# Image shift's product with the value weight: formed on VectorE and summed by a short strip, instead of a full strip on TensorE

## The chip, the cores and the metric

One core of a Trainium2 chip runs the whole kernel. The metric is device microseconds of one execution; the median of three runs of the kernel before is 116.47 us (116.44 to 116.78).

## The reference

One attention block of a diffusion transformer with two streams, image (2 x 256 tokens) and text (2 x 32 tokens), both of width D = 1152, all in bfloat16. `c` has one row for each of the two images of the batch (called image 0 and image 1 below).

```python
mod_i = (silu(c) @ wmod_img).reshape(B, 6, 1, D)      # mod_t likewise from wmod_txt
shi, sci, gai = mod_i[:, 0], mod_i[:, 1], mod_i[:, 2]  # shift, scale, gate
hi = layernorm(x_img) * (1 + sci) + shi               # ht likewise
qkvi = hi @ wqkv_img                                   # qkvt likewise
q, k, v = concat(text, image) of the three thirds
p = softmax(q @ k^T * D ** -0.5)
a = p @ v
out_i = x_img + gai * (a_img @ wo_img)                 # out_t likewise
```

What the change touches is a rearrangement of the value path. The kernel multiplies the value weight `w_v_i` with the normalized and scaled image tokens before the shift is added. The missing part of v is the same for all tokens of one image: the row `shi @ w_v_i`. Since each row of p sums to one, that row may be added once behind the attention (`sv`, added to `aT`), if the text's v has it subtracted (`v_t` and `svn`). So the kernel needs `shi @ w_v_i`: two rows of 1152 numbers, each a sum over 1152 products.

## The kernel before

Weights are 1152 x 1152 blocks, loaded as `[128, 9, 1152]` (a partition holds nine rows, indexed `kt`; 2.65 MB each). There are fourteen of them. They come in by DMAs that the SP queue issues in one fixed order, into six buffers of the pool `w` that are used in turn: a load waits on SP until the block that had its buffer is no longer read, and everything behind it on SP waits too. `w_sc_i` and `w_v_i` have two of the six buffers first.

The order of work is written out by hand, and each engine works through its own list:

- Start: layer norm of the image tokens, scale columns, and v without its shift (L244, L395, L344), until about 31.7 us. The image's shift is formed as a *strip* (below), read back as columns into `mod_i`, and added to `hT_i` (L223, L226, L230); the last evacuation of v on VectorE (L153) ends at 33.7 us.
- Query stage, `qk_img(w_q_i, 0)`: nine output blocks `j` of 128 columns, each nine matmuls of 512 tokens (L445). The first three blocks run together, the others one by one. `qk_evac` moves each block from PSUM to `qkT`, alternating between VectorE (L429) and ScalarE (L431).
- Three strips, L452 to L454: `tsh` (text shift, called the shift strip), `tsc` (text scale, the scale strip) and `svr` (the image shift's product with `w_v_i`, the third strip). A strip (`strip_rows`) multiplies two rows with a whole weight block. It uses only 32 of TensorE's columns at a time, so that four column groups take four pieces of the output side by side: 9 x 4 matmuls of 256 columns (L368) and 9 of 128 (L372), then one evacuation to SBUF by `evac`, which alternates between VectorE (L153) and ScalarE (L155). `svr` uses `shT32`, a copy of the shift columns that GpSimd makes. Behind it GpSimd negates a part (`svn`, L456) and issues six DMAs that spread the rows through DRAM (`ssc`) to the text partitions (`v_t`, L459 and L463).
- Key stage, `qk_img(w_k_i, 1, hooks)`: as the query stage. The hooks put other work ahead of a block: `txt_norm` ahead of block 0 (layer norm of the text `x_t` into `xn_t`, L162 to L174, then a table load for the exponential on ScalarE, L474), `all_cols` ahead of block 3 (the *selection*: six small matmuls, L384 and L386, turn the strips `tsh` and `tsc` into columns, and VectorE writes them to `mod_t`, L389 and L391), `txt_transposes` ahead of block 6 (nine small matmuls, L489, transpose the text; VectorE multiplies and adds into `hT_t`, L490 and L492).
- Text projections of query and key (L503), scores and softmax (L529, L516, L521), text scores and gate (L542), text value (L604), transposes of p, attention output (L673; `sv` is added in L686 and L688), output projection (L765), text output (L783), stores.

PSUM tiles of the tag `mm` take seven banks in turn: in the key stage a new block or strip can start only when the tile seven before it has been evacuated.

## Time and profile before

| | |
|---|---|
| runs, median of three | 116.47 us (116.44 to 116.78) |
| span of the profiled execution | 114.4 us |
| TensorE busy | 109.5 us, 96% of the span |
| VectorE, ScalarE, GpSimd busy | 53.3, 34.3, 27.9 us |
| DMA | 40.89 MB, 357 GB/s over the span, 396 to 416 GB/s from 20 to 94 us |
| TensorE clock granted | 1.00 throughout |

The profiled execution has no time of its own besides its span, from the first to the last instruction of the program; the runs' times lie 2.1 us above it (116.47 less 114.4). Times in the views are microseconds from the start of the span; mean durations of one instruction are nanoseconds. PE is TensorE's matmuls, PEld its weight loads, DVE VectorE, ACT ScalarE, POOL GpSimd, SP the queue that issues the loads. A line such as L445 is a line of the kernel file.

### The profile page before, as it was taken

To read this page: it belongs to the slowest core of one execution; us is meant where nothing else is said; L and a number is where in the kernel's file an instruction comes from. 1 tells how busy PE (TensorE), PEld (TensorE's weight loads), DVE (VectorE), ACT (ScalarE), POOL (GpSimd) and SP (SyncE) were. 2 spreads that over 40 slices of the span, in tenths; PEclk is the share of its full clock that TensorE was granted. 3 is DMA by queue.
4 is the path that set the end of the run, shared out by engine and by line. 5 is a ranking of instruction groups with operands and counts; after the bars stand their busy time and mean duration, and the time that the engine had idled before them with its cause. 6 is when DMAs were issued, how large, how long until landed. Compare 5 with 4: busy or idle time off the path is not lost.

```text
span 114.4 us, 2934 instructions
## 1 busy us (share of the span) xinstructions
PE 109.5 (96%) x1248; PEld 65.7 (57%) x1255; DVE 53.3 (47%) x137; ACT 34.3 (30%) x84; POOL 27.9 (24%) x59
## 2 busy tenths in 40 slices
PE   5998999999999999999999999999999999999990
PEld 1364564544944444486444546987687565667670
DVE  1699820452470402211832342136665803998571
ACT  2829660342370321021360122116555700001000
POOL 7000102540140000002224000001450560999100
PEclk9999999999999999999999999999999999999999
DMA  3999999999999999999999999999999999962142
GB/s 72 347 389 323 366 380 401 413 412 413 413 405 404 412 413 405 409 412 410 405 408 413 396 411 413 404 416 399 412 407 406 407 413 397 389 241 103 39 156 69
DMA packets 22744, 40.89 MB, mean 357 GB/s; under 512 B 1279, under 2 KB 6539, under 8 KB 22731
## 3 DMA queue, kind: packets, MB, share of 16 engines
q1 hardware_dynamic: 21648, 39.64, 90.8%
q0 software_dynamic: 608, 0.88, 2.1%
q10 hardware_dynamic: 475, 0.18, 0.7%
q8 instruction: 10, 0.16, 0.5%
q14 instruction: 3, 0.02, 0.1%
HBM read 39.36 MB, written 1.34 MB: 356 GB/s over the span
## 4 chain that ended last, share of the span: by engine, by line
PE 87%; DMA 7%; SPq 3%; issue 1%; DVE 0%
PE qkps L445 30%; PE ps L765 16%; PE va L244 10%; DMA w_sc_i<-in_wmod_img_dram 7%; PE aps L673 5%; PE ps L503 4%; PE sps L529 4%; PE gps L368 4%; PE ops L783 2%; PE ps L344 2%; SPq L93 2%; PE ps L395 2%; PE ps L604 2%; PE mps L204 1%; PE gps L738 1%; PE sps L542 1%
## 5 line engine op out<-in xcount | busy, mean ns | idle before, releaser
L445 PE MATMUL qkps<-hT_i,t 128*128 128x512 bf16 x158 | 35.4, 379 | 0.2
L445 PEld LDWEIGHTS <-t 128*128 128x128 bf16 x162 | 15.6, 98 | 18.3
L765 PE MATMUL ps<-t,aT 128*128 128x384 bf16 x99 | 16.4, 326 | 0.0
L765 PEld LDWEIGHTS <-aT 128*128 128x128 bf16 x117 | 11.0, 98 | 6.9 <-issue 0.5
L244 PE MATMUL va<-w_v_i,hT_i 128*128 128x512 bf16 x60 | 14.1, 378 | 0.2
L749 POOL TENSOR_TENSOR w_og<-t,gb 128x384 bf16<-128x384 bf16 x9 | 8.8, 1018 | 4.2 <-issue 4.2
L244 PEld LDWEIGHTS <-hT_i 128*128 128x128 bf16 x63 | 5.8, 97 | 6.5 <-POOL hT_i L228 0.5
L771 DVE TENSOR_TENSOR tmp<-ps,gb 128x384 bf16<-128x384 f32 x11 | 6.0, 549 | 6.1 <-DMA gb<-mod_scratch 4.4
L429 DVE TENSOR_SCALAR qkT<-qkps 128x512 bf16<-128x512 f32 x4 | 2.8, 692 | 11.6 <-PE qkps L445 11.6
L139 PE MATMUL wps<-wz 128*128 128x512 bf16 x16 | 6.3, 551 | 1.2 <-DVE wz L127 1.2
L162 DVE BATCH_NORM_STATS2 stats<-x_i 128x6 f32<-128x384 bf16 x12 | 5.9, 538 | 2.6 <-DMA x_i<-in_x_img_dram 2.6
L431 ACT ACTIVATE qkT<-qkps 128x512 bf16<-128x512 f32 x5 | 2.9, 596 | 13.5 <-PE qkps L445 13.5
L153 DVE CAST qkT<-qkps 128x512 bf16<-128x512 f32 x4 | 2.8, 692 | 7.7 <-PE qkps L445 7.7
L228 POOL TENSOR_SCALAR hT_i<-hT_i,mod_img 128x256 bf16<-128x256 bf16 x5 | 2.5, 514 | 15.6 <-DVE mod_img L213 12.3
L155 ACT CAST qkT<-qkps 128x512 bf16<-128x512 f32 x5 | 2.8, 587 | 10.6 <-PE qkps L445 10.6
L523 POOL COPY px<-pb 128x64 bf16<-128x64 bf16 x4 | 0.9, 238 | 19.8 <-DVE pb L521 19.8
L772 DVE TENSOR_TENSOR o<-tmp,x_i 128x384 bf16<-128x384 bf16 x11 | 5.4, 488 | 0.4
L456 POOL TENSOR_SCALAR svn<-svr 128x128 bf16<-128x128 bf16 x1 | 0.3, 300 | 20.6 <-DVE svr L153 20.6
L686 DVE TENSOR_SCALAR aT<-aps,sv 128x288 bf16<-128x288 f32 (+2 forms) x11 | 4.3, 456 | 2.0 <-PE aps L673 2.0
L503 PEld LDWEIGHTS <-t 128*128 128x128 bf16 x162 | 4.9, 98 | 0.2
L503 PE MATMUL ps<-hT_t,t 128*128 128x64 bf16 x162 | 4.9, 193 | 0.0
L673 PE MATMUL aps<-pT,v_i 128*128 128x288 bf16 (+2 forms) x44 | 4.8, 264 | 0.0
(159 smaller groups left out, 143.8 us busy)
## 6 DMA issues: line engine op xcount, KB each, us to landing
t<-in_wmod_txt_dram SPq DMA_DIRECT2D x3, 2592.0 KB, 21.5
t<-in_wmod_img_dram SPq DMA_DIRECT2D x2, 2592.0 KB, 22.3
t<-in_wqkv_img_dram SPq DMA_DIRECT2D x6, 864.0 KB, 13.6
t<-in_wqkv_txt_dram SPq DMA_DIRECT2D x2, 2592.0 KB, 17.2
t<-in_wqkv_txt_dram SPq DMA_DIRECT2D x3, 864.0 KB, 13.6
t<-in_wo_img_dram SPq DMA_DIRECT2D x1, 2592.0 KB
t<-in_wo_txt_dram SPq DMA_DIRECT2D x3, 864.0 KB, 15.5
w_v_i<-in_wqkv_img_dram SPq DMA_DIRECT2D x4, 576.0 KB, 8.2
```

The costliest lines, as they stand in the source:

```text
L139: nc.tensor.matmul(ps[:], lhsT=wz[:, 0:P], rhs=wz[:], start=True, stop=True)
L162: nc.vector.bn_stats(stats[0:np_, k, :], x_ap[:, k * CH:(k + 1) * CH])
L244: nc.tensor.matmul(ps[:], lhsT=hT_i[:, kt, i * P:(i + 1) * P], rhs=w_v_i[:, kt, half * VW:(half + 1) * VW], start=(kt == 0), stop=(kt == K ...
L368: nc.tensor.matmul(gps[32 * g:32 * g + 32, 0:RC], lhsT=lhs[:, kt, :], rhs=wt[:, kt, g * RC:(g + 1) * RC], start=(kt == 0), stop=(kt == KT ...
L445: nc.tensor.matmul(pss[j - j0][:], lhsT=wq[:, kt, j * P:(j + 1) * P], rhs=hT_i[:, kt, :], start=(kt == 0), stop=(kt == KT - 1))
L503: nc.tensor.matmul(ps[:, j - j0, :], lhsT=wq[:, kt, j * P:(j + 1) * P], rhs=hT_t[:, kt, :], start=(kt == 0), stop=(kt == KT - 1))
L529: nc.tensor.matmul(sps[:], lhsT=qkT[:, ft, b, q0:q0 + P], rhs=qkT[:, KT + ft, b, :], start=(ft == 0), stop=(ft == KT - 1))
L673: nc.tensor.matmul(bank[:, off:off + c1 - c0], lhsT=lhsT, rhs=rhs, start=(first[id(bank)] == n), stop=(final[id(bank)] == n))
L749: nc.gpsimd.tensor_mul(w_og[:, dt, 0:CH], w_o_i[:, dt, NG0:D], gb[:, B - 1, NG0:D])
L765: nc.tensor.matmul(ps[:, 0:cw], lhsT=aT[:, dt, t0:t0 + P], rhs=rhs, start=(dt == DTS[0]), stop=(dt == DTS[-1]))
L771: nc.vector.tensor_mul(tmp[:, 0:cw], ps[:, 0:cw], gb[:, b, cs])
L772: nc.vector.tensor_add(o[:, cs], tmp[:, 0:cw], x_i[:, i, cs])
```

## The change

The third strip is replaced. VectorE multiplies row block `kt` of `w_v_i` with the shift column of that block, one scalar per partition, and adds up over `kt` in float32: for each image nine instructions on `[128, 1152]`, the first a product alone (`tensor_scalar`), the other eight a product and a sum (`scalar_tensor_tensor`). What is left is a sum over the 128 partitions. The sum `sacc` is split into a bfloat16 high part (a copy on ScalarE) and a low part (the difference, on VectorE), and `shift_strip` adds up both parts of both images over the partitions with a stationary operand of ones: 16 matmuls of 256 columns and 4 of 128, instead of 36 and 9.

All products of image 0 and two of image 1 stand in VectorE's list ahead of the query stage's evacuations, which are all given to ScalarE; the low part of image 0 and the other seven products of image 1 stand between query and key stage. The high part of image 0 stands on ScalarE ahead of query block 5; that of image 1 ahead of the key evacuations.

The strips move from before the key stage to ahead of its block 6 (hook 6: `tsh`, `tsc`, short strip, then `svn` and the six DMAs). `txt_norm` moves from block 0 to block 3, and the low part of image 1 is formed inside it; the text is normalized in place. The selection moves from block 3 to block 7, and the text transposes from block 6 to block 8, the last.

`w_v_i`, which is now read until the products end, gets a home of its own ("V"), which `w_ga_i` takes over afterwards; the pool `w` has five buffers instead of six. `w_k_i` is loaded ahead of `w_sh_t` and `w_sc_t` instead of behind them. `qkT` becomes two tiles; the key's shares its place with `sacc` of image 0. Several small tiles share places, and paddings keep the large homes at multiples of 256 bytes.

```diff
-    wpool = ctx.enter_context(tc.tile_pool(name="w", bufs=6))
+    wpool = ctx.enter_context(tc.tile_pool(name="w", bufs=5))
...
-    w_v_i = wpool.tile([P, KT, D], bf, tag="w", name="w_v_i")
+    w_v_i = act.tile([P, KT, D], bf, tag="V", name="w_v_i")
...
-    nc.gpsimd.tensor_copy(shT32[:, :, 0:B], mod_i[:, 0:KT, :])
-
+    w_k_i = load_w(wqkv_img, D, K3)
     w_sh_t = load_w(wmod_txt, 0)
     w_sc_t = load_w(wmod_txt, D)
-    w_k_i = load_w(wqkv_img, D, K3)
...
-    w_ga_i = load_w(wmod_img, 2 * D)
+    w_ga_i = load_w(wmod_img, 2 * D, home="V")
...
-    qkT = act.tile([P, 2 * KT, B, NTOK], bf, tag="Q")
+    saccs = [act.tile([P, D], f32, tag=t, name="sacc") for t in ("K", "sacc")]
+    qkTs = [act.tile([P, KT, B, NTOK], bf, tag="Q", name="qT")]
     def qk_evac(out_ap, in_ap, blk):
         if blk == 0:
-            if evac_idx[0] % 2 == 0:
-                nc.vector.tensor_scalar_mul(out_ap, in_ap, SCALE)
-            else:
-                nc.scalar.mul(out_ap, in_ap, SCALE)
-            evac_idx[0] += 1
+            nc.scalar.mul(out_ap, in_ap, SCALE)
...
+    def shift_products(b, k0, k1):
+        for kt in range(k0, k1):
+            ap = mod_i[:, kt, b:b + 1]
+            if kt == 0:
+                nc.vector.tensor_scalar(saccs[b][:], w_v_i[:, kt, :], ap, None, op0=ALU.mult)
+            else:
+                nc.vector.scalar_tensor_tensor(saccs[b][:], w_v_i[:, kt, :], ap, saccs[b][:], op0=ALU.mult, op1=ALU.add)
+    def shift_high(b):
+        sparts[0, b] = work.tile([P, D], bf, tag="o", bufs=3, name="shi")
+        nc.scalar.copy(sparts[0, b][:], saccs[b][:])
+    def shift_low(b):
...
+        nc.vector.tensor_sub(lo[:, 0:D], saccs[b][:], sparts[0, b][:])
+    def shift_strip():
+        gps = ps_mm.tile([P, RC + P], f32, tag="mm")
+        terms = [(n, b) for b in range(B) for n in range(2)]
+        for m, (n, b) in enumerate(terms):
+            for g in range(NGG):
+                nc.tensor.matmul(gps[32 * g:32 * g + 32, 0:RC], lhsT=ones32[:, b, :], rhs=sparts[n, b][:, g * RC:(g + 1) * RC],
+                                 start=(m == 0), stop=(m == len(terms) - 1), tile_position=(0, 32 * g))
+        for g, (n, b) in enumerate(terms):
+            nc.tensor.matmul(gps[32 * g:32 * g + 32, RC:RC + P], lhsT=ones32[:, b, :], rhs=sparts[n, b][:, NGG * RC:D],
+                             start=True, stop=True, tile_position=(0, 32 * g))
+        g_sb = work.tile([P, RC + P], bf, tag="svr", bufs=1, name="svr")
+        evac(g_sb[:], gps[:])
+        return g_sb
...
-    qk_img(w_q_i, 0, hooks={})
-    tsh = rows_for_cols(w_sh_t, "tsh")
-    tsc = rows_for_cols(w_sc_t, "tsc")
-    svr = rows_for_cols(w_v_i, "svr", lhs=shT32)
+    shift_products(0, 0, KT)
+    shift_products(1, 0, 2)
+    qk_img(w_q_i, 0, hooks={5: lambda: shift_high(0)})
+    shift_low(0)
+    shift_products(1, 2, KT)
+    shift_high(1)
+    qkTs.append(act.tile([P, KT, B, NTOK], bf, tag="K", name="kT"))
...
+    def row_strips():
+        strips["tsh"] = rows_for_cols(w_sh_t, "tsh")
+        strips["tsc"] = rows_for_cols(w_sc_t, "tsc")
+        svr = strips["svr"] = shift_strip()
...
     def txt_norm():
-        ln_apply(x_t[:, :], P, xn_t[:, :], *ln_std(ln_stats(x_t[:, :], P), P))
+        lns = ln_std(ln_stats(x_t[:, :], P), P)
+        shift_low(1)
+        ln_apply(x_t[:, :], P, x_t[:, :], *lns)
...
-    qk_img(w_k_i, 1, hooks={0: txt_norm, 3: all_cols, 6: txt_transposes})
+    qk_img(w_k_i, 1, hooks={3: txt_norm, 6: row_strips, 7: all_cols, 8: txt_transposes})
```

More of the change, by code (lines that the diff above doesn't have):

```diff
@@ L71, in w_view, with load_w @@
         return src.rearrange("(kt p) n -> p kt n", p=P)
-    def load_w(src, c0, ksplits=((0, KT),)):
-        t = wpool.tile([P, KT, D], bf, tag="w")
+    def load_w(src, c0, ksplits=((0, KT),), home=None):
+        t = wpool.tile([P, KT, D], bf, tag="w", name="t") if home is None else act.tile([P, KT, D], bf, tag=home, name="w_home")
         for (k0, k1) in ksplits:
@@ L129 @@
     nc.gpsimd.memset(sT32[:], 0.0)
-    shT32 = const.tile([P, KT, 32], bf)
-    nc.gpsimd.memset(shT32[:], 0.0)
+    ones_full = const.tile([P, B * 32 + 96], bf)
+    ones32 = ones_full[:, 0:B * 32].rearrange("p (b c) -> p b c", b=B)
+    nc.gpsimd.memset(ones32, 0.0)
+    for b in range(B):
+        nc.gpsimd.memset(ones32[:, b, b:b + 1], 1.0)
     sTw_full = const.tile([P, KT * NT + 96], bf)
@@ L377, in rows_for_cols @@
         gps = strip_rows(wt, sT32 if lhs is None else lhs)
-        g_sb = work.tile([P, RC + P], bf, tag=nm, bufs=1, name=nm)
+        g_sb = work.tile([P, RC + P], bf, tag={"shr": "svr", "tsc": "garow2", "tsh": "of"}[nm], bufs=1, name=nm)
         evac(g_sb[:], gps[:])
@@ L422 @@
     gsc = tc.dram_tile([B, D], bf, name="mod_scratch")
-    qkT = act.tile([P, 2 * KT, B, NTOK], bf, tag="Q")
+    saccs = [act.tile([P, D], f32, tag=t, name="sacc") for t in ("K", "sacc")]
+    qkTs = [act.tile([P, KT, B, NTOK], bf, tag="Q", name="qT")]
     def qk_evac(out_ap, in_ap, blk):
         if blk == 0:
-            if evac_idx[0] % 2 == 0:
-                nc.vector.tensor_scalar_mul(out_ap, in_ap, SCALE)
-            else:
-                nc.scalar.mul(out_ap, in_ap, SCALE)
-            evac_idx[0] += 1
+            nc.scalar.mul(out_ap, in_ap, SCALE)
         else:
             evac(out_ap, in_ap)
+    sparts = {}
+    def shift_products(b, k0, k1):
[9 more added lines that the diff above has]
+    def shift_low(b):
+        if b == 0:
+            lo = work.tile([P, D], bf, tag="o", bufs=3, name="slo")
+        else:
+            lo_full = act.tile([P, D + 32], bf, name="slo_full")
+            lo = lo_full[:, 0:D]
+        sparts[1, b] = lo
+        nc.vector.tensor_sub(lo[:, 0:D], saccs[b][:], sparts[0, b][:])
[12 more added lines that the diff above has]
+        return g_sb
     def qk_img(wq, blk, hooks):
@@ L447, in qk_img @@
             for j in range(j0, j1):
-                qk_evac(qkT[:, blk * KT + j, :, 0:NI], pss[j - j0][:].rearrange("p (b n) -> p b n", b=B), blk)
-    qk_img(w_q_i, 0, hooks={})
-    tsh = rows_for_cols(w_sh_t, "tsh")
-    tsc = rows_for_cols(w_sc_t, "tsc")
-    svr = rows_for_cols(w_v_i, "svr", lhs=shT32)
+                qk_evac(qkTs[blk][:, j, :, 0:NI], pss[j - j0][:].rearrange("p (b n) -> p b n", b=B), blk)
+    shift_products(0, 0, KT)
[5 more added lines that the diff above has]
+    qkTs.append(act.tile([P, KT, B, NTOK], bf, tag="K", name="kT"))
     svn = const.tile([P, P], bf)
-    nc.gpsimd.tensor_scalar(svn[:], svr[:, RC:RC + P], -1.0, 0.0, op0=ALU.mult, op1=ALU.add)
     ssc = tc.dram_tile([B, NM], bf, name="shift_scratch")
-    for b in range(B):
-        nc.gpsimd.dma_start(ssc[b, :].rearrange("(q j) -> q j", q=NGG), svr[b:P:32, 0:RC])
-    for g in range(2):
-        for b in range(B):
-            r = 32 * (2 * g + b)
-            nc.gpsimd.dma_start(v_t[r:r + NT, :], ssc[b, g * VW:(g + 1) * VW].partition_broadcast(NT))
+    strips = {}
+    def row_strips():
+        strips["tsh"] = rows_for_cols(w_sh_t, "tsh")
+        strips["tsc"] = rows_for_cols(w_sc_t, "tsc")
+        svr = strips["svr"] = shift_strip()
+        nc.gpsimd.tensor_scalar(svn[:], svr[:, RC:RC + P], -1.0, 0.0, op0=ALU.mult, op1=ALU.add)
+        for b in range(B):
+            nc.gpsimd.dma_start(ssc[b, :].rearrange("(q j) -> q j", q=NGG), svr[b:P:32, 0:RC])
+        for g in range(2):
+            for b in range(B):
+                r = 32 * (2 * g + b)
+                nc.gpsimd.dma_start(v_t[r:r + NT, :], ssc[b, g * VW:(g + 1) * VW].partition_broadcast(NT))
     mod_t = const.tile([P, 2, KT, B], f32, name="mod_txt")
@@ L468 @@
     hT_t = act.tile([P, KT, NTT], bf)
-    xn_t = act.tile([P, D], bf)
     def txt_norm():
-        ln_apply(x_t[:, :], P, xn_t[:, :], *ln_std(ln_stats(x_t[:, :], P), P))
+        lns = ln_std(ln_stats(x_t[:, :], P), P)
+        shift_low(1)
+        ln_apply(x_t[:, :], P, x_t[:, :], *lns)
         junk = small.tile([P, 1], f32, bufs=1)
@@ L477, in all_cols @@
         ctp = ps_sm.tile([P, 2, NCOL + B], f32, tag="sm")
-        for k, rows in enumerate((tsh, tsc)):
+        for k, rows in enumerate((strips["tsh"], strips["tsc"])):
             select_cols(rows, ctp[:, k, :])
@@ L488, in txt_transposes @@
             for kt in range(k0, k1):
-                nc.tensor.matmul(tpt[:, kt - k0, :], lhsT=xn_t[:, kt * P:(kt + 1) * P], rhs=pick, start=True, stop=True)
+                nc.tensor.matmul(tpt[:, kt - k0, :], lhsT=x_t[:, kt * P:(kt + 1) * P], rhs=pick, start=True, stop=True)
             nc.vector.tensor_mul(hv[:, k0:k1], tpt[:, 0:k1 - k0, :].rearrange("p k (b t) -> p k b t", b=B),
@@ L504 @@
                                      start=(kt == 0), stop=(kt == KT - 1))
-            qk_evac(qkT[:, blk * KT + j0:blk * KT + j0 + jn, :, NI:NTOK],
+            qk_evac(qkTs[blk][:, j0:j0 + jn, :, NI:NTOK],
                     ps[:, 0:jn, :].rearrange("p j (b n) -> p j b n", b=B), blk)
@@ L528, in scores_img @@
         for ft in range(KT):
-            nc.tensor.matmul(sps[:], lhsT=qkT[:, ft, b, q0:q0 + P], rhs=qkT[:, KT + ft, b, :],
+            nc.tensor.matmul(sps[:], lhsT=qkTs[0][:, ft, b, q0:q0 + P], rhs=qkTs[1][:, ft, b, :],
                              start=(ft == 0), stop=(ft == KT - 1))
@@ L541, in scores_txt_and_gate @@
             for b in range(B):
-                nc.tensor.matmul(sps[NT * b:NT * (b + 1), :], lhsT=qkT[:, ft, b, NI:NTOK], rhs=qkT[:, KT + ft, b, :],
+                nc.tensor.matmul(sps[NT * b:NT * (b + 1), :], lhsT=qkTs[0][:, ft, b, NI:NTOK], rhs=qkTs[1][:, ft, b, :],
                                  start=(ft == 0), stop=(ft == KT - 1), tile_position=(0, NT * b))
@@ L582, in softmax_txt @@
         nc.vector.reduce_max(nmx[0:q, :], sps[0:q, :], axis=AX.X, negate=True)
-        e = work.tile([P, NTOK], f32, tag="e", bufs=1)
+        e = work.tile([P, NTOK], f32, tag="of", bufs=1, name="e")
         rs = small.tile([P, 1], f32, tag="rst", bufs=1)
@@ L629, in p_transposes @@
         svp = ps_sm.tile([P, NCOL + B], f32, tag="sm", name="svp")
-        select_cols(svr, svp)
+        select_cols(strips["svr"], svp)
         nc.vector.tensor_copy(pX[:], pX_ps[:, NT:NTOK + 2 * NT])
```

## The prediction

> **What bounds the kernel now.** I read the page's first part and the chain of waits by line, then the chain in order of time, then a table of stretches, then VectorE's groups by form and its timeline, and last the weight loads' issues.

> ```profile
> PE 109.5 (96%) x1248; PEld 65.7 (57%) x1255; DVE 53.3 (47%) x137; ACT 34.3 (30%) x84; POOL 27.9 (24%) x59
> ...
> PE 87%; DMA 7%; SPq 3%; issue 1%; DVE 0%
> ```

> TensorE is busy 96% of the span and is 87% of the chain that ended last; the DMA and SP shares (10%) lie before 12 us, where the first weights come in. What shortens the kernel is TensorE work taken away after that, as long as no new wait opens.

> The chain in order of time (start, length, what):

> ```profile
> 42.83 6.42 PE qkps L445 x29
> 49.25 1.10 PE gps L368 x36
> 50.35 0.16 PE gps L372 x9
> 50.51 0.98 PE gps L368 x36
> 51.49 0.11 PE gps L372 x8
> 51.60 0.98 PE gps L368 x30
> 52.59 0.22 PE gps L372 x8
> 52.80 0.76 PE qkps L445 x3
> ...
> 70.81 4.72 PE ps L503 x162
> ```

> The three strips fill 49.25 to 52.80 without a gap: 3.55 us, 1.18 each. In the table of stretches (us, then busy us of PE, PEld, DVE, ACT, POOL) TensorE is full before and behind them, while VectorE has room:

> ```profile
> 31.70:49.25 17.55, 17.44 (x85) 7.82 (x88) 4.76 (x13) 4.10 (x9) 1.15 (x3) 1.00 1.04 408
> ...
> 52.80:70.80 18.00, 17.89 (x101) 8.45 (x103) 7.56 (x18) 4.03 (x7) 3.63 (x7) 1.00 1.04 408
> ```

> The DMAs run at 408 GB/s all the while, so a load that starts late could become a second bound.

> **The strip.** Removed: the third strip, 36 matmuls of 256 columns and 9 of 128. Four column groups run side by side, so 36 are nine rounds: 0.98/9 to 1.10/9 = 0.11 to 0.12 us a round. Added: 16 matmuls of 256 columns (four rounds, 0.44 to 0.49) and 4 of 128 in one round (9 take 0.22 in three, so 0.07): about 0.53. TensorE saves 1.18 - 0.53 = **0.65 us**. The other two strips only move. Moving them puts three transitions elsewhere and adds none.

> **The products on VectorE.** 18 instructions of 1152 elements, and no row has one. The nearest, by form (operation, out<-in, count, busy us, mean ns of one):

> ```profile
> L162 DVE BATCH_NORM_STATS2 stats<-x_i 128x6 f32<-128x384 bf16 x12 | 5.9, 538 | 2.6 <-DMA x_i<-in_x_img_dram 2.6
> ...
> L686 DVE TENSOR_SCALAR aT<-aps,sv 128x288 bf16<-128x288 f32 x7 | 3.4, 511 | 2.0 <-PE aps L673 2.0
> ...
> L174 DVE TENSOR_SCALAR xn_i<-x_i,mv,rstd 128x1152 bf16<-128x1152 bf16 x4 | 2.3, 578 | 0.1
> ...
> L521 DVE TENSOR_SCALAR pb<-e,rs 128x288 bf16<-128x288 f32 x4 | 1.5, 370 | 0.1
> ...
> L573 DVE TENSOR_TENSOR v_t<-ps,v_t 128x512 bf16<-128x512 f32 x1 | 0.7, 692 | 0.2 <-PE ps L604 0.2
> ...
> L686 DVE TENSOR_SCALAR aT<-aps,sv 128x64 bf16<-128x64 f32 x2 | 0.6, 276 | 0.0
> ```

> L686 grows by (511-276)/224 = 1.05 ns an element and has 0.21 us fixed, with a scalar per partition; L573, without one, has 692 - 512x1.04 = 0.16. So an accumulating product (two inputs, one float32) is 1152x1.04 + 0.21 = 1.41 us. Each waits for the one before: L490's pair ends at 66.17 and the dependent L492 starts at 66.21, so 0.04 more and **1.45 us apart**. The first of each image has one input; L521, float32 in SBUF with such a scalar, takes 0.37 where L686 takes 0.51 at the same width, half the time per element, so 0.6 + 0.21 = 0.81. Bounds for the accumulating one: from 0.58 (L174, one 16-bit input) to 1.61 (L162 stretched, 1152 x 538/384). I take 1.45, because L686 and L573 share its one element per 1.04 ns, and keep 1.61 for the range.

> The subtraction that forms the low part has no scalar: 1.36. ScalarE's copy to the high part: L230, 496 for 256 from SBUF, plus 896 x 0.84 (its 512 against 256 wide reads of PSUM, 586 and 372) = 1.25.

> [...]

> **Does VectorE keep up?** On the profile's axis: the v evacuation ends at 33.7. Image 0's products end at 33.7 + 0.81 + 8x1.45 = 46.1; two of image 1 at 48.3; the low part waits for ScalarE's copy (47.4) and ends at 49.7; the last seven at 59.7 (three starts need no wait and overlap by 0.08, as the L686 do, eight of 3.48 us together in 2.89: 59.5). ScalarE copies until 60.8, and behind that copy in its queue stand the evacuations of key blocks 0 and 2 (61.4, 62.0). VectorE goes on with block 1 (60.2), text statistics (1.48, 0.24), the second low part (63.2), reciprocal and text normalization (0.74: 63.9), blocks 3 and 5, the scale strip's evacuation (0.56): 65.6.

> TensorE without a stall: key stage from 49.25, blocks 0 to 5 are 54 x 0.216 and end at 60.9; shift strip to 62.1, scale strip to 63.3, short strip to 63.85, block 6 to 65.8, selection, block 7 to 67.8, text transposes (0.27) to 68.1, block 8 to 70.0, text projections from about 70.15 instead of 70.81. Due against ready:
> - the scale strip takes the PSUM bank of block 0 (seven banks in turn): due 62.1, ready 61.4;
> - the short strip's fourth round reads the second low part: due 63.65, ready 63.2;
> - the selection reads the evacuated scale strip: due 65.8, ready 65.6;
> - the text product: transposes to `hT_t` took 0.36 + 1.60 from the first matmul to the end of L492 once VectorE is free: ready 69.8, due 70.0. Before it had three blocks of cover (5.8 us), now it has one (1.94).

> Everything is covered, but by 0.2 to 0.7 us. I count 0.1 us of stall. Were the cover gone, each 0.1 us on the spacing would cost 16 x 0.1 = 1.6 us.

> **Evacuations, ScalarE.** The query evacuations all go to ScalarE: nine at 0.60 in 17.5 us; the copy at 46.1 to 47.4 delays block 5 by 4 us with seven banks to hold it. In the key stage the table load (1.28) is passed by 63.6, then block 4 and the shift strip by 64.7, due at 65.8 at the earliest. Text evacuations change engines too: the second of the key's goes to VectorE, 0.36 (192 x 1.04 + 0.16) against 0.32, and the scores' first six steps (4.45 us for four blocks of nine: 0.12 each, 0.7) run before it is read. POOL loses a copy of 0.20 at 32.65. Nothing on the path.

> **Loads.** `w_k_i` moves ahead of two others: no part of it is needed before 49.25 and it lands 13 us earlier (two loads of 2.65 MB at 408 GB/s). `w_sh_t`, `w_sc_t` then land where its thirds did, by 54.4 (when `x_t` landed), due 60.9. The five-buffer ring and the home "V" change who frees what. `w_ga_i` waits for the products (59.5) instead of 49.25; `w_v_t` for the end of the key stage (70) instead of the strips, with all later weights queued behind it on SP:

> ```profile
> 51.83 6.28 SPq L76 DMA_DIRECT2D t<-in_wmod_img_dram  x1
> 58.20 9.52 SPq L76 DMA_DIRECT2D t<-in_wqkv_txt_dram  x3
> 67.82 4.16 SPq L76 DMA_DIRECT2D t<-in_wo_img_dram  x1
> ```

> The first of these landed 22.3 us after its issue, at 74.1, its data having started when `w_k_t` was in, near 67.8. An issue at 59.5 still precedes that. `w_v_t` issued at 70 has 4 us before the engines run dry, and the kernel's first load, on an empty queue, landed 3.0 us after its issue. So hidden; a gap of 1 us would show only at L604 (80.9), and `w_v_t` landed from 76.4 to 80.7 before. POOL's six shift DMAs move by about 11 us to 66 to 77, wanted at 83; its queue then waits there until 71, ahead of work at 78. Nothing again.

> **Homes.** In both built programs the weights' homes lie at multiples of 256 bytes; smaller tiles shift by 64 or 128 bytes. The strips' matmuls take 272 to 273 ns from each home that the trace shows, so this is costed at nothing; a gain or loss would show in that number.

> **The sum.** -0.65 + 0.1 = -0.55 on the profiled span of 114.4; the runs' median 116.47 is 2.1 longer, taken to stay. Forecast **115.9 us**. A measurement of this kernel tells some 0.3% (0.35 us) from no change.

> **Rivals.**
> - *VectorE is the bound* (slower). At 1.55 apart the stream is 1.6 us late and the selection, which everything behind stands on, waits that less its 0.2 of margin, 1.4: 116.47 - 0.65 + 1.4 = 117.2; at 1.61, 118.2. It decides from 1.46 on, and from 1.50 the gain is gone. For it: margins of 0.2 us behind a chain of 26 us, a duration without a row. Against it: the rows at one element a step all have 1.04 to 1.05 ns, whatever the operation. Chance 0.23.
> - *The margins eat it* (no change that can be told). Spacing of 1.48, or 0.3 to 0.5 us at the one-block cover of the text product: 116.3. Chance 0.18.
> - [...] Chance 0.02. [...]
> - *The late `w_v_t` opens a gap in the DMAs*: over 4 us between issue and first data would be needed, and L604's matmuls would then wait the rest: 117. Chance 0.02.

> The forecast holds 0.55. Faster 0.55, same 0.18, slower 0.27. The range runs from 115.6 (full saving, a little more per round) to 117.4, where the first rival with a spacing of 1.56 ends; likeliest case alone: 115.6 to 116.1.

> **What would show it.** Right: chain without strips at 49.25; a short strip of 0.5 to 0.6 us; products of about 1.41 us, 1.45 apart, ending near 59.5; text projections near 70.1 to 70.3. Wrong: idle TensorE before the scale strip, the selection or the text projections (L503, in the changed file L548), or products over 1.46 apart; the text value matmuls (L604) waiting for a DMA.

## The result and the profile after

The change made the kernel slower: 117.54 us (median of 22 runs) against 116.77 us (22 runs of the kernel before on the same chip), a ratio of 1.0066 with an interval of [1.005, 1.0081], so about 0.77 us lost where 0.55 was to be won. The forecast of 115.9 missed in sign, and 117.54 lies outside its range. Medians are over all runs, while ratios and intervals leave out disturbed executions such as the one of 287.64 us in which the changed kernel's first profile fell, so the views shown here are those of a second profile of the same file (117.67 us against 116.86, ratio 1.0061 [1.0037, 1.0084]; span 115.8 us).

From the page, the busy times of the engines and the queues of the DMAs (queue: packets, MB, share):

```profile
PE 109.3 (94%) x1230; PEld 64.8 (56%) x1230; DVE 76.2 (66%) x152; ACT 38.6 (33%) x91; POOL 27.7 (24%) x60
...
q8 instruction: 9, 0.15, 0.5%
```

TensorE has less to do and a longer span around it, so a gap has opened on it. VectorE went from 47% to 66%. The last row is small and easily passed over: it is the queue that the page names "instruction", with nine packets here. In the page of before it has ten.

The chain in order of time (start, length, what) from the query stage to the scores:

```profile
32.41 29.14 PE qkps L481 x135
61.55 1.10 PE gps L371 x36
62.64 0.16 PE gps L375 x9
62.80 0.98 PE gps L371 x36
63.78 0.11 PE gps L375 x8
63.90 0.44 PE gps L463 x13
64.33 0.11 PE gps L466 x3
64.44 2.05 PE qkps L481 x9
...
68.86 1.94 PE qkps L481 x9
70.80 4.55 PE ps L548 x156
75.35 1.29 issue
76.64 0.35 PE ps L548 x6
76.99 4.41 PE sps L574 x36
```

None of the waits that the prediction listed occurred: fifteen blocks run without a break, the three strips follow each other without a wait, the short one takes 0.54 us (63.90 to 64.44), and the text projections begin at 70.80 without having waited for `hT_t`. Then, in the middle of these projections, behind 156 of 162 matmuls, TensorE stands still for 1.29 us, and "issue" means that it waits for nothing that the profile shows. The list of TensorE's waits between 60 and 80 us (line, releaser, us in total, times, longest) has this one entry, where the kernel before has none:

```profile
PE ps L548 <- issue: 1.3, 1, 1.3
```

The account against a second profile of the kernel before (116.85 us, span 114.8, query stage from 32.21, text projections 71.26 to 75.98): from the start of the query stage to the text projections 38.39 instead of 39.05 us, so -0.66; the text projections 6.19 instead of 4.72, +1.47 (the stop, and six matmuls that take 0.35 behind it); the scores 4.41 instead of 4.45. The sum is +0.77, what the runs say.

VectorE's products, by form (count, busy us, mean ns of one, idle before them), and a table of stretches (busy us of PE, PEld, DVE, ACT, POOL, then clock, DMA share, GB/s):

```profile
L443 DVE SCALAR_TENSOR_TENSOR sacc<-w_v_i,mod_img,sacc 128x1152 f32<-128x1152 bf16 x16 | 22.7, 1418 | 0.5
...
L441 DVE TENSOR_SCALAR sacc<-w_v_i,mod_img 128x1152 f32<-128x1152 bf16 x2 | 1.6, 808 | 0.0
```

```profile
31.70:49.25 17.55, 17.55 (x92) 8.29 (x90) 17.21 (x22) 7.75 (x16) 1.61 (x3) 1.00 1.04 408
...
70.80:77.00 6.20, 4.91 (x164) 4.77 (x161) 0.69 (x1) 1.30 (x3) 1.99 (x4) 1.00 1.05 401
```

VectorE is full in the query stage (17.21 of 17.55 us), and TensorE runs beside it without a gap. In the last stretch TensorE is busy 4.91 of 6.20 us, at a granted clock of 1.00, and every other engine is mostly idle.

### The profile page after: what moved, and what is told of

It reads as the page before. It is cut to its first block, busy times and chain, and to the rows that moved or that the text cites. A ratio compares the mean times of both kernels' runs of the same rounds, so it can differ in the third digit from the quotient of the medians.

```text
span 285.6 us, 2918 instructions
## 1 busy us (share of the span) xinstructions
PE 281.7 (99%) x1230; PEld 125.1 (44%) x1230; DVE 76.3 (27%) x152; ACT 40.1 (14%) x91; POOL 27.0 (9%) x60
## 4 chain that ended last, share of the span: by engine, by line
PE 99%; DVE 0%; issue 0%
PE qkps L481 34%; PE ps L810 17%; PE va L247 13%; PE aps L718 5%; PE ps L548 4%; PE sps L574 4%; PE wps L142 3%; PE gps L371 3%; PE ops L828 2%; PE ps L649 2%; PE ps L398 2%; PE tp L190 2%; PE ps L347 2%; PE gps L783 1%; PE mps L207 1%; PE sps L587 1%
## 5 line engine op out<-in xcount | busy, mean ns | idle before, releaser
L481 PE MATMUL qkps<-hT_i,t 128*128 128x512 bf16 x162 | 97.2, 834 | 0.0
L481 PEld LDWEIGHTS <-t 128*128 128x128 bf16 x162 | 27.8, 174 | 65.0 <-issue 64.1
L810 PE MATMUL ps<-t,aT 128*128 128x384 bf16 x99 | 44.4, 682 | 0.0
L247 PE MATMUL va<-w_v_i,hT_i 128*128 128x512 bf16 x63 | 38.3, 828 | 0.0
L810 PEld LDWEIGHTS <-aT 128*128 128x128 bf16 x117 | 19.5, 170 | 28.7 <-issue 27.4
L443 DVE SCALAR_TENSOR_TENSOR sacc<-w_v_i,mod_img,sacc 128x1152 f32<-128x1152 bf16 x16 | 22.7, 1419 | 0.5
L548 PEld LDWEIGHTS <-t 128*128 128x128 bf16 x162 | 12.2, 144 | 0.9 <-issue 0.9
L548 PE MATMUL ps<-hT_t,t 128*128 128x64 bf16 x162 | 12.2, 282 | 0.0
L574 PE MATMUL sps<-kT,qT 128*128 128x288 bf16 x36 | 12.2, 571 | 0.0
L718 PE MATMUL aps<-pT,v_i 128*128 128x288 bf16 (+2 forms) x44 | 12.2, 508 | 0.0
L371 PE MATMUL gps<-t,sT 128*32 128x256 bf16 x108 | 8.5, 517 | 0.0
```

The source lines that it names most:

```text
L247: nc.tensor.matmul(ps[:], lhsT=hT_i[:, kt, i * P:(i + 1) * P], rhs=w_v_i[:, kt, half * VW:(half + 1) * VW], start=(kt == 0), stop=(kt == K ...
L371: nc.tensor.matmul(gps[32 * g:32 * g + 32, 0:RC], lhsT=lhs[:, kt, :], rhs=wt[:, kt, g * RC:(g + 1) * RC], start=(kt == 0), stop=(kt == KT ...
L443: nc.vector.scalar_tensor_tensor(saccs[b][:], w_v_i[:, kt, :], ap, saccs[b][:], op0=ALU.mult, op1=ALU.add)
L481: nc.tensor.matmul(pss[j - j0][:], lhsT=wq[:, kt, j * P:(j + 1) * P], rhs=hT_i[:, kt, :], start=(kt == 0), stop=(kt == KT - 1))
L548: nc.tensor.matmul(ps[:, j - j0, :], lhsT=wq[:, kt, j * P:(j + 1) * P], rhs=hT_t[:, kt, :], start=(kt == 0), stop=(kt == KT - 1))
L574: nc.tensor.matmul(sps[:], lhsT=qkTs[0][:, ft, b, q0:q0 + P], rhs=qkTs[1][:, ft, b, :], start=(ft == 0), stop=(ft == KT - 1))
```

## The experiments

Three theories stood at first, named as in the expectations: "VectorE" (its long stream, or what stands behind it, comes late), "loads" (the homes and the order of the loads cost the time) and "place" (the text projections wait, now that they have one block of cover). The profile above speaks against the last as it stood, since the stop is within the projections and not ahead of them; that TensorE's own instructions come late came up behind these runs. All times are medians, each against the kernel before on the same chip.

**The changed kernel again** (no edit), for the profile above.

> The changed kernel once more, for a trace without disturbance: 117.3 to 117.8 us. The forecast missed about 1.3 us (a gain of 0.55 was expected, a loss of 0.8 was measured). Theory VectorE: idle TensorE of 1.2 to 1.5 us in the key stage, ahead of the scale strip, the short strip or the selection, because the products or what stands behind them on VectorE and ScalarE come late. Theory place: the idle time is ahead of the text projections (one block of cover). Theory loads: TensorE waits for a weight DMA somewhere behind 70 us, or at the start of the key stage.

117.67 us, 1.0061 [1.0037, 1.0084]. The loss is there again, and the stop with it.

**One product for each image instead of nine** (sixteen of the eighteen products are left out, so the row `shi @ w_v_i` is incomplete):

```diff
-        for kt in range(k0, k1):
+        for kt in range(k0, min(k1, 1)):
```

> Of the 18 products only the first of each image is left (the image shift's product is incomplete). Theory VectorE: the stream ends 16 x 1.45 = 23 us earlier, no wait is left in the key stage, and the short strip's saving shows: 115.8 to 116.2 against a kernel before of 116.5 to 116.8. Theories place and loads: as slow as the changed kernel, 117.3 to 117.8.

117.55 us, 1.0054 [1.0034, 1.0075]; span 115.8. The chain at the same place:

```profile
70.79 4.55 PE ps L548 x156
75.33 1.36 issue
```

With 22 us of VectorE's work gone, the stop stands where it stood, behind the same 156 matmuls. VectorE isn't the cause, and sixteen products more or less make no difference that can be measured (117.67 and 117.55 us).

**Homes and loads alone** (the kernel before, with five buffers, the home "V" for `w_v_i` and then `w_ga_i`, and `w_k_i` loaded first; strips where they were):

```diff
-    wpool = ctx.enter_context(tc.tile_pool(name="w", bufs=6))
+    wpool = ctx.enter_context(tc.tile_pool(name="w", bufs=5))
...
+    w_k_i = load_w(wqkv_img, D, K3)
     w_sh_t = load_w(wmod_txt, 0)
     w_sc_t = load_w(wmod_txt, D)
-    w_k_i = load_w(wqkv_img, D, K3)
...
```

> The kernel before with only the homes and the order of the loads of the change (five buffers, a home V for the value weight and then the gate weight, the key weight ahead of the text's shift and scale). Theory loads: slower than before by 0.8 us or more. Theories VectorE and place: as before, within 0.3%.

122.66 us, 1.0379 [1.0315, 1.0442]. The chain says why, and that this was a poor test:

```profile
32.42 0.11 PE qkps L445
32.53 22.15 DMA t<-in_wmod_txt_dram
54.68 0.04 issue
54.72 1.17 PE gps L368 x36
```

The strips, still ahead of the key stage, now wait until 54.7 for a weight that comes later. The new order of loads and the late strips belong together; taken apart they tell nothing of the whole. The text projections of this trace run without a stop.

**Late strips without products** (the kernel above, with the three full strips, the text norm, the selection and the text transposes at the new places):

```diff
...
-    qk_img(w_k_i, 1, hooks={0: txt_norm, 3: all_cols, 6: txt_transposes})
+    qk_img(w_k_i, 1, hooks={3: txt_norm, 6: row_strips, 7: all_cols, 8: txt_transposes})
```

> As loads_only, and the three full strips, text norm, selection and text transposes moved to the key blocks where the change has them; no products on VectorE. Theory place: 0.6 us or more slower than loads_only, with idle TensorE ahead of the text projections. Theory VectorE: like loads_only within 0.2 us, since the same TensorE work only stands elsewhere.

120.23 us, 1.0244 [1.0201, 1.0287]:

```profile
70.58 0.77 DVE hT_t L495
71.34 0.14 issue
71.48 4.13 PE ps L506 x131
75.61 2.29 issue
77.90 1.42 PE ps L506 x31
```

Two things are lost here. The text is not ready in time (`hT_t` ends at 71.34, so there are waits of about 2 us ahead of 71.48), and then comes a stop in the text projections, longer than the changed kernel's. (The granted clock is 1.00 up to the end of the stop and 0.58 from 77.90 to 82.00, so only what follows is stretched.) So the stop needs neither the products nor the short strip. It comes behind 131 matmuls, not 156; and the full third strip is 25 matmuls with their weight loads (50 instructions) longer than the short one. The stop stands at the same instruction of TensorE's list: the text projections begin at instruction 1212 here and at 1162 in the changed kernel (all of TensorE's instructions counted from 0 in the built program), and 1212 + 2 x 131 = 1162 + 2 x 156 = 1474.

This brought up the queue "q8 instruction". Its packets have 16,384 bytes; nine come in for the 2473 instructions of TensorE's list, ten for the 2523 of the padded one below, so about 256 instructions each (an estimate from these counts). In the changed kernel one packet starts at 74.31, 1.04 us ahead of the stop, and TensorE goes on 2.33 us behind its start.

**25 small matmuls more** (the changed kernel, with two-column matmuls behind the warm-up, while TensorE waits for the first weights; they give the list its old length of 50 more):

```diff
+    def tiny(n):
+        ps = ps_mm.tile([P, VW], f32, tag="mm", name="tps")
+        for _ in range(n):
+            nc.tensor.matmul(ps[:, 0:2], lhsT=wz[:, 0:P], rhs=wz[:, 0:2], start=True, stop=True)
...
     warm(11)
+    tiny(25)
```

> The changed kernel with 25 more matmuls of two columns at the start, where TensorE is idle; the text projections then stand at TensorE's instruction 1212, as in the kernel before, instead of 1162. In the changed kernel's trace TensorE stops for 1.29 us inside the text projections, at its instruction 1474, waiting for nothing but a 16 KB packet of the instruction queue that starts 1.0 us before. Theory position (what counts is only where in TensorE's list the 256-instruction pieces end): the stop goes, 116.2 to 116.4. Theory read-ahead (the piece that is missing is asked for when TensorE's sequencer passes instruction 1218, and the sequencer stands at the text projections' first instruction, 1212, until the text is ready): it is asked for at 70.4, no earlier than in the changed kernel, and the stop stays or grows: 117.5 to 118.1.

118.54 us, 1.0155 [1.0122, 1.0189]. The stop moved by just these 25 matmuls, and grew:

```profile
70.75 3.82 PE ps L554 x131
74.57 1.96 issue
76.53 1.08 PE ps L554 x31
```

The packet starts at 74.21, about as late as in the changed kernel (74.31), while TensorE reaches instruction 1474 by 0.8 us earlier. The old length of the list does not bring the old time back: with the text as late as here, something else delays the packet.

**33 small matmuls** (the same edit with `tiny(33)`):

> As pad25 with 33 matmuls: the text projections begin at instruction 1228, behind 1218. Theory position: no stop, 116.2 to 116.4. Theory read-ahead: the sequencer passes 1218 in the last key block, before the wait; no stop, 116.2 to 116.4. Theory chance (the stop has another cause, such as the DMA traffic of that moment): as the changed kernel, 117.4 to 117.8.

116.25 us, 0.9962 [0.9946, 0.9979]; span 114.1. Eight more matmuls, and the stop is gone:

```profile
68.60 1.94 PE qkps L487 x9
70.54 4.72 PE ps L554 x162
75.27 4.41 PE sps L580 x36
```

This version beats both kernels: the one before by 0.44 us by the ratio (0.24 to 0.63; the medians lie 0.31 apart) and the changed one by more than 1 us.

**29 small matmuls** (`tiny(29)`), to see where it turns:

> As pad33 with 29 matmuls: the text projections begin at instruction 1220, two behind 1218. With 25 (1212) the stop grew to 1.96 us, with 33 (1228) it was gone. Theory read-ahead, with the request at 1218: no stop, like pad33, 0.3 to 0.5% faster than before. If the request comes from elsewhere between 1212 and 1228 (or takes effect some instructions later), the stop is still there: 117.5 to 118.5.

118.31 us, 1.0123 [1.0095, 1.0151]:

```profile
70.80 3.70 PE ps L554 x127
74.50 1.93 issue
```

With the text projections from instruction 1220 the stop is there, with 1228 it isn't; it is a threshold here, no slope (1.96 us at 1212, 1.93 at 1220, none at 1228). The stop stands at 1220 + 2 x 127 = 1474 again. The guess that the piece is asked for at 1218 was wrong by a few instructions: if the request is what turns here, it comes from an instruction between 1220 and 1228.

**The kernel before, its list lengthened by 206 instructions** (the strips and everything else as before; 109 small matmuls in place of six warm-up matmuls, so that the text projections begin at 1418, which is 256 behind the changed kernel's 1162):

```diff
-    warm(11)
+    warm(5)
+    tiny(109)
```

> The kernel before with 109 matmuls of two columns in place of 6 of the 16 that warm TensorE up: its text projections begin at instruction 1418, 256 beyond the changed kernel's 1162, so that pieces end at the same places in it; nothing else is changed. Theories position and read-ahead: a stop of 1.0 to 1.7 us inside the text projections, 117.8 to 118.5 against 116.8. Theory chance: 116.6 to 117.0.

119.8 us, 1.0275 [1.0231, 1.0318]. A part of this was not wanted: the query stage begins 1.9 us later (34.10 instead of 32.21). The rest is the stop, in a kernel that has nothing of the change in it. At 1.83 us it is longer than the 1.0 to 1.7 expected:

```profile
73.15 4.55 PE ps L509 x156
77.70 1.83 issue
79.53 0.35 PE ps L509 x6
```

It comes behind 156 matmuls again, at 1418 + 312 = 1730 = 1474 + 256: one piece further on. That fixes the size of a piece at 256 instructions, and the counts of packets fit: with an end of a piece at 1474 and every 256 from there, nine lie below 2473, and a tenth, 2498, below 2523. The packet starts at 76.99. The text was not late here: `hT_t` is ready at 69.30, 3.85 us ahead of the projections, just as in the kernel before.

**The kernel before again** (no edit): 116.85 us, one run, for a second trace of it.

> The kernel before once more, for a second trace: the query stage began at 31.6 in its first one and at 32.1 to 32.2 in four traces of changed kernels. If that is only the run, it begins anywhere from 31.5 to 32.3 here too, and no gap of TensorE over 0.5 us lies behind 32 us.

No gap of more than 0.5 us on TensorE behind 32 us. Its packet starts at 71.30 and instruction 1474 is due at 75.08 (131 pairs of 29.1 ns from 71.26 on), 3.78 us later. In the changed kernel TensorE goes on 2.33 us behind the packet's start, so by an estimate from these two the piece was there 1.5 us in time. Its query stage begins at 32.21, not at 31.77 as in the first trace, so part of the changed kernel's 0.2 to 0.6 us later beginning is spread between executions. Whether all of it is isn't settled: nine traces with the new order of loads begin between 32.16 and 32.42, three with the old order at 31.77, 31.82 and 32.21. The 0.31 to 0.44 us that 33 small matmuls win by the runs are less than the 0.66 us saved behind this point.

**33 small matmuls and one product:**

> pad33 with only the first product of each image (the image shift's product is incomplete). Theory hidden: the 16 products cost nothing, equal to pad33 within 0.15 us. Theory VectorE (the products still cost something that the chain does not show): 0.2 us or more faster than pad33.

116.25 us, 0.9963 [0.9945, 0.9981], the same as with all products. Without the stop, too, the products cost nothing that can be measured.

**Homes alone** (the kernel before with five buffers and the home "V", its old order of loads and strips):

```diff
-    wpool = ctx.enter_context(tc.tile_pool(name="w", bufs=6))
+    wpool = ctx.enter_context(tc.tile_pool(name="w", bufs=5))
...
-    w_v_i = wpool.tile([P, KT, D], bf, tag="w", name="w_v_i")
+    w_v_i = act.tile([P, KT, D], bf, tag="V", name="w_v_i")
...
-    w_ga_i = load_w(wmod_img, 2 * D)
+    w_ga_i = load_w(wmod_img, 2 * D, home="V")
```

> The kernel before with only the pool of five buffers and the home V for the value weight and then the gate weight; the loads' order is that of before. pad33 gained 0.31 to 0.44 us by its runs where its trace against a second one of before shows 0.68. Theory homes: the first weights come in later from the new homes, and this kernel is 0.2 to 0.4 us slower than before. Theory runs: equal to before within 0.15 us, and the rest is the spread of the first loads from run to run.

116.51 us, 0.9987 [0.9967, 1.0008]: no difference that can be told, and no stop (its packet starts at 70.64).

**25 small matmuls, the text one block earlier** (the kernel with the 1.96 us stop; only the hook of the text transposes is moved):

```diff
-    qk_img(w_k_i, 1, hooks={3: txt_norm, 6: row_strips, 7: all_cols, 8: txt_transposes})
+    qk_img(w_k_i, 1, hooks={3: txt_norm, 6: row_strips, 7: lambda: (all_cols(), txt_transposes())})
```

> pad25 with the text transposes ahead of key block 7 (right behind the selection) instead of block 8: the text is ready for the projections near 69.2 instead of 70.3, with two blocks of cover instead of one. The instruction list before the text projections is as long as in pad25 (they begin at 1212). Theory read-ahead (the missing piece is asked for when the wait for the text ends, 3.8 to 3.9 us before its packet): the packet starts near 73.1 instead of 74.2 and the stop shrinks by 1.1, from 1.96 to about 0.9; 117.3 to 117.6. Theory position (only the place in the list counts): the stop stays at 1.9 to 2.0 and the time at 118.3 to 118.6.

117.12 us, 1.0046 [1.0024, 1.0067]:

```profile
70.59 3.82 PE ps L554 x131
74.41 0.79 issue
75.20 1.08 PE ps L554 x31
```

No instruction was added or taken away, and the text projections begin at the same instruction, 1212; the transposes stand one block earlier in the list. `hT_t` is ready earlier, at 68.97 instead of 70.34, though TensorE never waited for it in either kernel. The packet starts 1.24 us earlier (72.97) and the stop is 1.17 us shorter. The time came out 0.2 us below what was expected, the stop about as expected.

The kernels side by side, times in us from the traces; "first" is the instruction at which the text projections begin and "begin" when they do; "due" is when TensorE reaches the first instruction of the piece, counted at 29.1 ns a pair where there is no stop:

| kernel | first | begin | text ready | packet starts | after text ready | due | goes on |
|---|---|---|---|---|---|---|---|
| before, second trace | 1212 | 71.26 | 67.41 | 71.30 | 3.89 | 75.08 | no stop |
| before, homes alone | 1212 | 70.86 | 67.02 | 70.64 | 3.62 | 74.67 | no stop |
| before, homes and loads | 1212 | 75.20 | 71.36 | 74.97 | 3.61 | 79.01 | no stop |
| changed | 1162 | 70.80 | 70.38 | 74.31 | 3.93 | 75.35 | 76.64 |
| changed, one product | 1162 | 70.79 | 70.37 | 74.33 | 3.96 | 75.33 | 76.69 |
| late strips | 1212 | 71.48 | 71.33 | 75.46 | 4.13 | 75.61 | 77.90 |
| 25 more | 1212 | 70.75 | 70.34 | 74.21 | 3.87 | 74.57 | 76.53 |
| 25 more, early text | 1212 | 70.59 | 68.97 | 72.97 | 4.00 | 74.41 | 75.20 |
| 29 more | 1220 | 70.80 | 70.39 | 74.16 | 3.77 | 74.50 | 76.43 |
| 33 more | 1228 | 70.54 | 70.13 | 69.78 | before it | 74.12 | no stop |
| before, 206 more | 1418 | 73.15 | 69.30 | 76.99 | 7.69 | 77.70 | 79.53 |

From the first row to "29 more" the packet starts 3.6 to 4.1 us after the text is ready, at whatever time that is. In every row with a stop TensorE goes on 2.2 to 2.5 us after the packet's start, and the stop is there just in the rows whose packet starts less than that ahead of due (0.1 to 1.4 us; in the others 3.8 us or more). The last row breaks the first rule. There the stream of TensorE's instructions passed its wait for `hT_t` early, as the row of that wait shows (PEldq is TensorE's queue of instructions; the last two times are the first and last start), below it the changed kernel's:

```profile
L509 PEldq EVENT_SEMAPHORE  x1: 51/51/51, 69.3 to 69.3; - x1
...
L548 PEldq EVENT_SEMAPHORE  x1: 51/51/51, 70.4 to 70.4; - x1
```

Still the packet starts 7.69 us behind that, which is 3.84 us behind the beginning of the projections; in the changed kernel, at the same place against the pieces, it is 3.51 us behind it. So two things can make a piece late. Where the projections begin at 1212, close to where the piece is asked for, an early text brings it earlier: 25 more with and without early text show that. Where they begin 50 instructions ahead of that (1162, and 1418 one piece further on), an early text didn't prevent the stop.

The stretch uses its instructions up quickly: in the second trace of the kernel before 324 of them pass in 4.72 us, so by an estimate from this a piece of 256 in 3.7 us, while from the end of the wait for the text to the end of the stop it is 6.0 to 6.6 us in the kernels that begin at 1162 to 1220.

## Why the prediction was wrong

**The gain was right.** From the query stage to the text projections 0.66 us are saved, with 0.65 predicted, and 33 small matmuls leave that gain standing (32.16 to 70.54: 38.38 instead of 39.05). The text projections begin at 70.80 instead of the 70.15 predicted, because the query stage begins at 32.41 and not at 31.77 as in the first profile.

**VectorE was right.** A product takes 1418 ns (1.41 predicted), eight of them 11.60 us (1.45 apart), the first of each image 0.81, the low parts 1.35 and 1.30 (1.36), ScalarE's copy 1.15 (1.25). The stream ends at 60.19; 59.5 was predicted from a start at 33.7, and it started at 34.26 in this trace. Successive products stand 0.03 apart (1.45 less 1.418; 0.04 predicted). That VectorE becomes the bound did not happen: TensorE had no idle time in the key stage, and leaving sixteen products out changed nothing that can be measured (117.67 and 117.55 us).

**The due times were right as far as they went.** The scale strip's evacuation (65.46 to 66.0) is ready for the selection at 66.38; the text product is ready at 70.38, and the first text projection's matmul starts at 70.64 (70.80 in the chain, when the matmul ahead of it ends).

**The loads: right in effect, wrong in one step.** `w_v_t` was to be issued at 70, at the end of the key stage; its DMAs were issued from 62.83, right behind the shift strip (62.80), whose weight had the same buffer. The profile's SP timeline (start, us, what):

```profile
60.22 0.37 SPq L76 DMA_DIRECT2D w_home<-in_wmod_img_dram  x1
62.83 4.62 SPq L76 DMA_DIRECT2D t<-in_wqkv_txt_dram  x3
```

No matmul behind 32 us waits for a load. The homes alone cost nothing that can be told, as taken (116.51 us, 0.9987 of the kernel before).

**The step that failed** is "Everything is covered, but by 0.2 to 0.7 us. I count 0.1 us of stall." The list of due times behind it asks only when a matmul reads data; that TensorE's own instructions could be due later than they come was put at nothing, without a reason. The reads were in time. What came late, by 1.29 us, is the piece of instructions that begins at 1474, and the text projections took 6.19 us instead of 4.72: the missing term of the sum is +1.47 us.

Two parts of the change bear on that term, and the prediction counted for each only the work and the waits for data. The cover of the text product was cut from three blocks (5.8 us) to one (1.94): the wait for `hT_t` was over 3.8 us ahead of the first text projection before (67.41 against 71.26), and is now over 0.4 us ahead (70.38 against 70.80). And 50 instructions were taken out ahead of the projections, which moved them from 1212 to 1162. Each alone was enough for a stop in some run: the late text with the projections at 1212 (1.96 us, 25 more), and the changed kernel's place against the pieces with the text 3.85 us early (1.83 us, the kernel before with 206 more). By the latter, if it carries over, an early text would not have saved the changed kernel; which of the two makes its 1.29 us stays open. The rival "the margins eat it" named the one-block cover of the text product, but with a late operand as its mechanism and a price of 0.3 to 0.5 us; no rival had TensorE's own instructions in it.

The prediction's list of signs helped: "idle TensorE before ... the text projections" would have been the mark of a late text. The gap was within them instead, behind 156 of 162 matmuls, and this is what told a late operand from a late instruction.

## What to carry to other kernels

In a dense stretch of small matmuls (here 29 ns for a weight load and a matmul) TensorE can use up its instructions before the next piece of them is there, even where no matmul waits for data (stops of 0.79 to 2.29 us here). Two things moved the piece here: at which instruction the stretch begins, and, where it began at 1212, how early the wait ahead of it was over. Operands that are ready early are therefore not enough: 3.85 us of cover did not help at 1418. If "issue" idle time stands in the middle of a run of equal matmuls, count instructions from the start of the list: a stop at the same number in several versions, or 256 further, was a late piece of instructions here (at 1474 in six kernels, at 1730 in one), and a few small matmuls in idle time at the start can move the stretch against the boundaries (33 here, with the query stage from 32.16, within the spread of the other traces; 109 in place of six warm-up matmuls made it begin 1.9 us later). Test a restructuring's parts only in combinations that its loads allow, and read the stop's place before its size.

## What the hardware showed that was not expected

- TensorE can stand still for 0.79 to 2.29 us for lack of instructions, all operands ready and no semaphore to wait for; the page shows it only as "issue" and as a queue with 0.5% of the DMA time.
- A threshold within four small matmuls (29 against 33 of them, over 60 us ahead of the stop) makes about 2 us of difference in the run times (1.0123 and 0.9962 of the kernel before).
- Sixteen float32 accumulations of 1418 ns beside TensorE at full rate cost no time that can be measured: 116.25 us with and without them.
